# A fused attention and two-layer MoE kernel: the last six w1 tiles decoded two keys later and written into the ring, sums of tokens moved to VectorE, first copies to ScalarE

## The chip, the cores and the metric

The kernel runs on one core of a Trainium2 chip. Its engines work side by side, each through its own list of instructions in order: TensorE (PE, matrix products, with its weight loads shown as PEld), VectorE (DVE), ScalarE (ACT), GpSimd (POOL) and SyncE (SP), which issues the DMAs here. Results of TensorE land in PSUM, in eight banks, and are read from there by VectorE or ScalarE. The metric is the device time of one execution in microseconds (us), as a median over runs.

## The reference

```python
def reference(q, k, v, w1, b1, w2, moe_*, moe2_*):
    # attention: 4 batches, 8 heads, 576 positions, 64 per head
    bias = relu(log-relative position @ w1 + b1) @ w2
    a = softmax(q @ k.T / 8 + bias) @ v          # -> x: 2304 tokens x 512
    # MoE1: 512 -> 768 -> 512
    h = np.maximum(np.maximum(x @ moe_w1, x @ moe_w2), x @ moe_w3)
    x = h @ moe_w_out
    # MoE2: 512 -> 2048 -> 512
    h = x @ moe2_w_in
    g = np.where(h > 0, h, np.exp(np.minimum(h, 0)) - 1)
    return g @ moe2_w_out
```

The weights of both MoE layers are float64 on input. The tokens and weights of the MoE layers are each split into a high and a low half, so that one product of the reference is three matmuls (high by high, high by low, low by high).

## The kernel before, in words

Attention fills roughly the first third of the time, MoE1 comes next, MoE2 after it. The text below is on the stretches that the change touches.

**Decoding weights.** A weight tile (128 x 512 numbers of 64 bits) comes from DRAM as `raw` (`fetch`, L346, two buffers), is put together to float32 by five VectorE instructions (L395, L398, L400, L402, L405) and one of ScalarE (L397) in `decoder`, and is split in `split` into a high half (ScalarE, `hi_of`, L74) and a low half (POOL, `lo_of`, L80). The list `DQ` (L330 to L334) gives the order of the tiles, called keys here: 18 tiles of w1 (the three inputs' matrices of MoE1, six blocks m by three matrices w), six of `wo` (MoE1's output), then those of MoE2 (`wi`, `w3`). Tiles of `wo` stay in SBUF. A tile of w1 normally goes to a buffer `sp`, from there by a store to DRAM (`scw_w_m_w`, L441, issued when another one is queued, in `store`), and, each time it is needed, by a load from there (`load_w`, L468) into a ring `wr` of six buffers `w_t`. There is one exception: where the key is the very next one to be loaded and the ring has room (`direct` in `split`), the halves are written straight into the ring; the key is noted in `HERE`, and its `load_w` issues no DMA. It is stored all the same, for the later passes.

**MoE1** makes three passes over the w1 tiles, one for each 768 tokens, 18 steps each. A step (L600 to L616) calls `load_w` for the tile four steps ahead, `moe1_mm` (24 matmuls, L495) and `moe1_ev`, which evicts the product from PSUM (ScalarE copy L505, VectorE maximum L507) and pumps the decoder, one key a step. There are four pairs of PSUM banks, so the product of step i waits for the eviction of step i-4.

**MoE2** goes through 24 units, eight slices of the hidden layer for three blocks of 768 tokens; the matrix products of the units after the second use sums and differences of token parts (`comb`: `first` computes `e`, L652, and `d`, L653; then d + e, L655; the high half, ScalarE; the low half, VectorE, L80), so that fewer matmuls are needed. In the first two units (n < 2) the sums aren't there yet, and each unit does four plain products, called q here, of 12 matmuls (L666), in turn into the banks Y and X (`bk`). Each q is followed by a copy `c_t` out of PSUM, a `step` for the pieces of ELU that wait (L696 on VectorE; then the high half `gh` on ScalarE and the low half `gl` on POOL, L80), `elu` (Relu, L688, and Exp, L689, on ScalarE), in the second unit by output products of the unit before (three groups of three matmuls, L710), and by two of the sixteen functions of the four sums. From the third unit on, copies and sums `p1`, `c11`, `q1` take products out of the banks; the sums for blocks 1 and 2 are made on the way, in eight more combs.

**The end of a block.** `store_out` copies the six accumulators of output (128 tokens x 512) from PSUM to SBUF, on VectorE and ScalarE in turn, and issues the DMA to `out` (L719); the sixth is copied and stored in two halves.

The order within these stretches is that of the code (`tc.manual_schedule`).

Of the kernel before, what the change touches and what calls it, by code (L numbers as in the profile page):

```python
# [15 lines left out]
ALU = mybir.AluOpType  # L16
# [36 lines left out]
def fused_kernel(ctx, tc, tkq, vv, lt, pk, wm1, wo1, win2, wo2, out):  # L53
    nc = tc.nc
# [15 lines left out]
    def hi_of(eng, dst, src):  # L70
        if eng == "p":
            nc.gpsimd.tensor_scalar(dst, src, 1.0, 1.0, op0=ALU.mult, op1=ALU.mult)
        elif eng == "a":
            nc.scalar.activation(dst, src, AF.Copy)  # L74
        else:
            nc.vector.tensor_copy(dst, src)  # L76

    def lo_of(eng, dst, src, hi):
        e = nc.gpsimd if eng == "p" else nc.vector
        e.tensor_tensor(out=dst, in0=src, in1=hi.bitcast(F32), op=ALU.subtract)  # L80
# [43 lines left out]
    with ExitStack() as pro:  # L124
# [18 lines left out]
        with tc.manual_schedule():  # L143
# [38 lines left out]
            for A in range(36):  # L182
# [9 lines left out]
                o = bt.tile([128, 576], F32, tag="o", name="o_t")  # L192
# [5 lines left out]
                c, r = divmod(A, 8)  # L198
# [130 lines left out]

    DQ = []  # L330
    w1s, wos = [("w1", m, w) for m in range(NM1) for w in range(3)], [("wo", kk, 0) for kk in range(NM1)]
    DQ += w1s[:12] + wos[:3] + w1s[12:] + wos[3:]
    for f in range(NU):
        DQ += [("wi", f, 1), ("wi", f, 0), ("w3", f, 0), ("w3", f, 1)]  # L334
    RAW = {}
# [17 lines left out]
    SCW, WO, HERE, WS, WN = {}, [], set(), [], [0, 0]  # L353
# [75 lines left out]
    todo, late = [], []  # L429

    def splits():

        for fn in late.pop(0) if late else ():
            fn()

    def store():
        if not todo:
            return
        key, sp2, c0 = todo.pop(0)
        d = dram.tile([128, 2, 512], F32, name=f"scw_{key[0]}_{key[1]}_{key[2]}")  # L440
        nc.sync.dma_start(d[:, :, c0:], sp2.bitcast(F32)[:, :, c0:])  # L441
        SCW[key] = d

    dec = decoder()
# [6 lines left out]
    def need(key):  # L451
        while key not in SCW:
            if any(k[0] == key for k in todo):
                store()
            elif late:
                splits()
            else:
                next(dec)

    def load_w(key):  # L460
        need(key)
        if key in HERE:
            HERE.remove(key)
            return
        WN[0] += 1
        t = wr.tile([128, 2, 512], F32R, tag="w", name="w_t")
        c0 = 256 if key[0] == "wi" and key[2] == 3 and key[1] > 1 else 0
        nc.sync.dma_start(t.bitcast(F32)[:, :, c0:], SCW[key][:, :, c0:])  # L468
        WS.append((key, t))

    def take_w(key):
        k, t = WS.pop(0)
        WN[1] += 1
        assert k == key
        return t[:, 0], t[:, 1]
# [44 lines left out]
    for s, (n, c) in enumerate(steps):  # L520
        o = {nm: s + off for nm, off in OFF.items()}
# [48 lines left out]
    for i, (blk, f) in enumerate(units + [(3, 0)]):  # L570
        a = [("wi", f, p) for p in range(4)] if blk < 3 else []
        w = [("w3", units[i - 1][1], p) for p in range(2)] if i else []
# [65 lines left out]
    def x_part(blk, j, t):  # L638
        t0 = blk * TB + t * NB
        return tuple(z[:, 2 * j:2 * j + 2, t0:t0 + NB] for z in (XH, XL))  # L640

    def comb(blk, i):
        a = partial(x_part, blk, *{1: (0, 1), 2: (1, 1), 3: (1, 1), 4: (1, 0)}[i])
        b = {1: partial(x_part, blk, 0, 0), 2: lambda: TT[blk, 1], 3: partial(x_part, blk, 0, 1),
             4: lambda: TT[blk, 2]}[i]
        tt, f = nc.vector.tensor_tensor, F32

        def first():
            t = mp.tile([128, 2, 2, NB], F32R, tag=f"t{i}", name=f"tt{i}", bufs=2 if i < 4 else 1)
            d, e = (mp.tile([128, 2, NB], F32, tag=g, name=f"{g}_t", bufs=1) for g in "de")  # L650
            x, y = a(), b()
            nc.gpsimd.tensor_tensor(out=e, in0=x[1].bitcast(f), in1=y[1].bitcast(f), op=ALU.subtract)  # L652
            tt(out=d, in0=x[0].bitcast(f), in1=y[0].bitcast(f), op=ALU.subtract)  # L653
            TT[blk, i] = (t[:, 0], t[:, 1])
            fns[1:] = [lambda: tt(out=d, in0=d, in1=e, op=ALU.add), lambda: hi_of("a", t[:, 0], d),  # L655
                       lambda: lo_of("v", t[:, 1], d, t[:, 0])]

        fns = [first, None, None, None]
        return [lambda j=j: fns[j]() for j in range(4)]
# [9 lines left out]
    def small(tag, bufs):  # L669
        return mp.tile([128, NB], F32, tag=tag, name=f"{tag}_t", bufs=bufs)  # L670

    def keep(tag, ps, eng):
        t = small(tag, 1)
        hi_of(eng, t, ps)
        return t
# [23 lines left out]
    def step():  # L699
        for p in [p for p in pend]:  # L700
            p.pop(0)()
            if not p:
                pend.remove(p)
# [8 lines left out]
    def store_out(blk, t):  # L712
        o = mp.tile([128, 512], F32, tag="o", name="o_t", bufs=4)
        r0 = blk * TB + 128 * t
        w = 256 if t == 5 else 512
        for c0 in range(0, 512, w):
            cs = slice(c0, c0 + w)
            hi_of("a" if t % 2 else "v", o[:, cs], acc[t][:, cs])
            nc.sync.dma_start(out[r0:r0 + 128, cs], o[:, cs])  # L719

    acc = PAIR[0] + PAIR[1] + PAIR[2]
# [10 lines left out]
    with tc.manual_schedule():  # L732
        for n, u in enumerate(units + [None]):
            pre = units[n - 1] if n else None
            if u:
                blk = u[0]
                GT[u] = [(mp.tile([128, TB], F32R, tag=f"gh{i}", name="gh"), mp.tile([128, TB], F32R, tag=f"gl{i}", name="gl"))
                         for i in range(2)]
                B11, B12, B21, B22 = (x_part(blk, j, t) for j in range(2) for t in range(2))
            if n < 2:  # L740

                for i in range(2):
                    w = take_w(("wi", u[1], 3 * i))
                    v = take_w(("w3", pre[1], i)) if pre else None
                    for q, (b, d) in enumerate(((B11, B21), (B12, B22))):
                        ps = (Y, X)[q]
                        prod(ps, w, 0, b, True, False)
                        prod(ps, w, 1, d, False, True)
                        c = small("c", 4)
                        hi_of("v", c, ps)  # L750
                        step()
                        elu(u, i, q, c)
                        if pre:
                            outs(pre, i, range(3 * q, 3 * q + 3), v)
                        for _ in range(2):
                            sums.pop(0)()
                    loads(2 if pre else 1)
                continue
            if u is None:
                for i in range(2):  # L760
                    step()
                    outs(pre, i, range(6), take_w(("w3", pre[1], i)))
                continue
            w = take_w(("wi", u[1], 0))
            prod(Y, w, 0, B11, True, False)
            p1 = keep("p1", Y, "v")
            step()
            v = take_w(("w3", pre[1], 0))
            outs(pre, 0, (0, 1), v)
            prod(X, w, 1, B21, True, True)  # L770
            loads(1)
            c11 = plus(X, p1)
            step()
            elu(u, 0, 0, c11)
            outs(pre, 0, (2, 3), v)
            w = take_w(("wi", u[1], 1))
            prod(Y, w, 0, TT[blk, 2], False, False)
            q1 = keep("q1", Y, "v")
            step()
            outs(pre, 0, (4, 5), v)  # L780
            loads(1)
            prod(X, w, 1, TT[blk, 1], True, False)
            p5 = keep("p5", X, "a")
            step()
            loads(1)
            v = take_w(("w3", pre[1], 1))
            outs(pre, 1, (0,), v)
            w = take_w(("wi", u[1], 2))
            prod(Y, w, 0, TT[blk, 3], False, False)
            u3 = keep("u3", Y, "v")  # L790
            step()
            outs(pre, 1, (1,), v)
            prod(X, w, 1, B22, False, True)
            c12 = plus(X, q1)
            step()
            elu(u, 0, 1, c12)
            c22 = plus(u3, p5)
            outs(pre, 1, (2, 3), v)
            w = take_w(("wi", u[1], 3))
            prod(Y, w, 1, TT[blk, 4], False, True)  # L800
            c21 = small("c", 4)
            hi_of("v", c21, Y)
            step()
            elu(u, 1, 1, c22)
            elu(u, 1, 0, c21)
            outs(pre, 1, (4, 5), v)
            loads(3)
            if blk < 2:
                if u[1] >= NU - 4:
                    pend.append(comb(blk + 1, u[1] - NU + 5))  # L810
# [65 lines left out]
```

## Time and profile before

| | |
|---|---|
| median of three runs | 1024.46 us (1024.25, 1024.46, 1029.13) |
| profiled execution, device time | 1025.84 us |
| its span, first to last instruction | 1023.9 us |
| mean granted clock of TensorE | 0.994 |
| TensorE busy | 1003.1 us (98%) |
| VectorE, ScalarE, POOL busy | 701.9, 547.5, 353.1 us |
| first pass of MoE1 | its products end near 410.7 us |
| first two units of MoE2 | products and outputs from 635.4 to about 662.5 us |

An engine's busy time says what share of the span it works; where it stands idle, the list of waits names the instruction that waited and what released it. The chain of waits follows the end of the program backwards, at each step to what released the instruction. A granted clock of 1.00 is TensorE's full 2.4 GHz, 0.5 is 1.2 GHz; a value between is a mean of both over the stretch.

### The profile page before, as it was taken

What the parts mean: (1) busy time and instruction counts of PE and PEld (TensorE: products, weight loads), DVE (VectorE), ACT (ScalarE), POOL (GpSimd) and SP (SyncE); (2) the same over time, 40 slices, a digit from 0 to 9 for tenths busy, and PEclk for the clock granted to TensorE, in tenths of its full rate; (3) what the DMA queues carried; (4) which work ended last, traced back from release to release, by engine and by line L of the source; (5) the groups of instructions that cost most, each with busy time, mean ns of one, the idle gap of its engine ahead of it and who ended that gap; (6) DMA issues with size and microseconds to landing.
All of it is one profiled execution on the core that took longest, in us unless ns stands there. A gap on an engine that the chain in (4) does not pass through costs nothing.

```text
span 1023.9 us, 17230 instructions
## 1 busy us (share of the span) xinstructions
PE 1003.1 (98%) x6068; PEld 836.8 (82%) x6068; DVE 701.9 (69%) x1402; ACT 547.5 (53%) x1175; POOL 353.1 (34%) x319
## 2 busy tenths in 40 slices
PE   7999999999999998999999999999999999999998
PEld 3456666666667898999999999889889989989896
DVE  7967877877876698887987962844775356753332
ACT  8978888888886233333333331444445345453443
POOL 0013333333332343534443550522452233522222
PEclk9989999999999999999999999999999999999999
DMA  7741724536332378869977990346567555575562
GB/s 266 267 166 63 248 84 171 160 124 208 124 109 93 124 243 276 303 215 346 319 279 249 324 319 6 113 139 200 178 193 266 182 186 181 193 258 191 171 202 103
DMA packets 68597, 200.80 MB, mean 196 GB/s; under 512 B 9376, under 2 KB 16416, under 8 KB 68512
## 3 DMA queue, kind: packets, MB, share of 16 engines
q1 hardware_dynamic: 68512, 199.70, 57.5%
q8 instruction: 49, 0.80, 0.3%
q14 instruction: 36, 0.29, 0.1%
HBM read 151.31 MB, written 48.37 MB: 195 GB/s over the span
## 4 chain that ended last, share of the span: by engine, by line
PE 92%; DVE 3%; DMA 3%; ACT 1%; issue 0%; SPq 0%; ACTq 0%; DVEq 0%
PE bk L666 16%; PE pb L710 12%; PE pb L495 10%; PE bk L495 9%; PE pb L224 8%; PE bk L299 7%; PE bk L710 6%; PE bk L257 4%; PE bk L590 4%; PE pb L590 4%; PE bk L269 3%; PE pb L186 2%; PE pbb L186 2%; PE pb L226 2%; PE bk L302 2%; DMA scw_w<-sp 2%
## 5 line engine op out<-in xcount | busy, mean ns | idle before, releaser
L80 POOL TENSOR_TENSOR gl<-t_t,gh 128x384 fp32r<-128x384 f32 x96 | 109.0, 1146 | 245.2 <-ACT gh L74 240.0
L250 POOL TENSOR_SCALAR e_t<-e_t,st_t 128x576 f32<-128x576 f32 x64 | 65.8, 1028 | 224.0 <-DVE st_t L244 208.6
L233 DVE CUSTOM_DVE_ANT_0 e_t<-pb,b_t 128x576 f32<-128x576 f32 x144 | 104.0, 756 | 51.3 <-PE pb L224 33.4
L74 ACT ACTIVATE p<-bk 128x512 f32<-128x512 f32 (+2 forms) x224 | 99.0, 473 | 53.0 <-PE bk L257 52.5
L495 PE MATMUL pb<-xh,w_t 128*128 128x384 f32 x448 | 117.2, 337 | 3.8 <-DMA w_t<-scw_w 3.8
L710 PE MATMUL pb<-w_t,gh 128*128 128x512 f32 x384 | 120.1, 394 | 0.0
L238 ACT ACTIVATE e_t<-e_t,st_t 128x576 f32<-128x576 f32 x144 | 111.8, 776 | 1.8 <-DVE st_t L233 1.8
L688 ACT ACTIVATE t_t<-c_t 128x384 f32<-128x384 f32 x96 | 50.0, 521 | 112.6 <-DVE c_t L679 87.2
L495 PE MATMUL bk<-xh,w_t 128*128 128x384 f32 x416 | 108.9, 337 | 0.8 <-ACT xf L320 0.6
L666 PE MATMUL bk<-tt,w_t 128*128 128x384 f32 x528 | 107.4, 338 | 0.0
L666 PEld LDWEIGHTS bk<-tt,w_t 128*128 128x128 f32 x528 | 95.1, 188 | 7.5
L666 PE MATMUL bk<-xh,w_t 128*128 128x384 f32 x328 | 95.7, 338 | 3.6 <-DVE c_t L76 3.6
L495 PEld LDWEIGHTS pb<-xh,w_t 128*128 128x128 f32 x448 | 81.1, 188 | 4.8 <-issue 2.9
L224 PE MATMUL pb<-kq_t 64*128 64x288 f32 x512 | 83.1, 437 | 1.0 <-DVE st_t L233 1.0
L710 PEld LDWEIGHTS pb<-w_t,gh 128*128 128x128 f32 x384 | 71.1, 189 | 6.7
L495 PEld LDWEIGHTS bk<-xh,w_t 128*128 128x128 f32 x416 | 75.4, 188 | 1.2 <-ACT xf L320 0.7
L299 PE MATMUL bk<-p,tv_t 128*64 128x320 f32 (+1 forms) x512 | 76.0, 418 | 0.0
L710 PE MATMUL pb<-w_t,gl 128*128 128x512 f32 x192 | 75.7, 394 | 0.0
L495 PE MATMUL pb<-xl,w_t 128*128 128x384 f32 x224 | 75.2, 336 | 0.0
L74 ACT ACTIVATE gh<-t_t 128x384 fp32r<-128x384 f32 x96 | 48.9, 518 | 46.3 <-DVE t_t L696 46.3
L696 DVE SCALAR_TENSOR_TENSOR t_t<-t_t,c_t 128x384 f32<-128x384 f32 x96 | 71.2, 759 | 0.3 <-issue 0.3
L224 PEld LDWEIGHTS pb<-kq_t 64*128 64x128 f32 x512 | 46.2, 190 | 29.0 <-issue 9.7
(116 smaller groups left out, 2134.7 us busy)
## 6 DMA issues: line engine op xcount, KB each, us to landing
w_t<-scw_w SPq DMA_DIRECT2D x96, 512.0 KB, 4.4
w_t<-scw_wi SPq DMA_DIRECT2D x74, 512.0 KB, 4.2
scw_w<-sp SPq DMA_DIRECT2D x28, 512.0 KB, 5.7
scw_wi<-sp SPq DMA_DIRECT2D x26, 512.0 KB, 4.6
raw<-wo SPq DMA_DIRECT2D x22, 512.0 KB, 4.8
scr<-o_t SPq DMA_DIRECT2D x36, 288.0 KB, 3.8
kq_t<-tkq SPq DMA_DIRECT2D x16, 640.0 KB, 4.4
raw<-wm SPq DMA_DIRECT2D x18, 512.0 KB, 3.9
```

Source lines behind the costliest of these rows:

```text
L74: nc.scalar.activation(dst, src, AF.Copy)
L80: e.tensor_tensor(out=dst, in0=src, in1=hi.bitcast(F32), op=ALU.subtract)
L224: mm(PB[h][:, o], t[r, 640 + 128 * c:768 + 128 * c], t[r, k0:k0 + 288], start=True, stop=True)
L233: nc.vector.tensor_tensor_reduce(out=E[s][:, 576 * h:576 * h + 576], in0=PB[h][:, 224:800], in1=BT[n // 4, c, h], op0=ALU.add, op1=ALU.min ...
L238: nc.scalar.activation(e, e, AF.Exp, bias=st[:, h:h + 1], scale=-1.0, accum_out=st[:, 2 + h:3 + h])
L250: nc.gpsimd.tensor_scalar(e, e, r, 1.0, op0=ALU.mult, op1=ALU.mult)
L299: mm(XO[64 * h:64 * h + 64, 0:w], v[:, 128 * k + 64 * h:128 * k + 64 * h + 64], ps[h][:, k, :], start=(k == 0), stop=False, skip_group_che ...
L495: mm(ps[blk][:, 0:NB], wt[:, ks], xt[:, kk, t0:t0 + NB], start=(j == 0), stop=(j == 11))
L590: mm(ps[blk][:, 0:NB], WO[0][:, kk, wt, ms], xt[:, bs], start=(j == 0), stop=(j == 3 * NM1 - 1))
L666: mm(ps, w[wt][:, ks], b[xt][:, kk], start=(start and j == 0), stop=(stop and j == 5), skip_group_check=True)
L696: pend.append([lambda: nc.vector.scalar_tensor_tensor(out=t, in0=t, scalar=-1.0, in1=c, op0=ALU.add, op1=ALU.max), last])
L710: mm(acc[t], g[:, ts], w[k], start=(f == 0 and i == 0 and j == 0), stop=(f == NU - 1 and i == 1 and j == 2))
```

## The change

1. `DQ`: two `wo` tiles (3 and 4) are decoded ahead of w1's blocks m = 4 and 5, so these six tiles come two keys later. `load_w` no longer decodes on until a tile is stored; a tile in `HERE` is enough.
2. `comb`'s `e` is computed on VectorE, not on POOL (all twelve combs).
3. In the first two units of MoE2 the copies `c_t` go to ScalarE, and the sixteen functions of the sums are called one after each q in the first unit and three in the second, not two and two.
4. `store_out`: the fifth output tile is copied and stored in halves too; the first halves of the fifth and sixth go to VectorE, the second ones to ScalarE.

```diff
--- before.py
+++ after.py
@@ -329,7 +329,7 @@
 
     DQ = []
     w1s, wos = [("w1", m, w) for m in range(NM1) for w in range(3)], [("wo", kk, 0) for kk in range(NM1)]
-    DQ += w1s[:12] + wos[:3] + w1s[12:] + wos[3:]
+    DQ += w1s[:12] + wos[:5] + w1s[12:] + wos[5:]
     for f in range(NU):
         DQ += [("wi", f, 1), ("wi", f, 0), ("w3", f, 0), ("w3", f, 1)]
     RAW = {}
@@ -458,7 +458,13 @@
                 next(dec)
 
     def load_w(key):
-        need(key)
+        while key not in HERE and key not in SCW:
+            if any(k[0] == key for k in todo):
+                store()
+            elif late:
+                splits()
+            else:
+                next(dec)
         if key in HERE:
             HERE.remove(key)
             return
@@ -649,7 +655,7 @@
             t = mp.tile([128, 2, 2, NB], F32R, tag=f"t{i}", name=f"tt{i}", bufs=2 if i < 4 else 1)
             d, e = (mp.tile([128, 2, NB], F32, tag=g, name=f"{g}_t", bufs=1) for g in "de")
             x, y = a(), b()
-            nc.gpsimd.tensor_tensor(out=e, in0=x[1].bitcast(f), in1=y[1].bitcast(f), op=ALU.subtract)
+            tt(out=e, in0=x[1].bitcast(f), in1=y[1].bitcast(f), op=ALU.subtract)
             tt(out=d, in0=x[0].bitcast(f), in1=y[0].bitcast(f), op=ALU.subtract)
             TT[blk, i] = (t[:, 0], t[:, 1])
             fns[1:] = [lambda: tt(out=d, in0=d, in1=e, op=ALU.add), lambda: hi_of("a", t[:, 0], d),
@@ -712,10 +718,10 @@
     def store_out(blk, t):
         o = mp.tile([128, 512], F32, tag="o", name="o_t", bufs=4)
         r0 = blk * TB + 128 * t
-        w = 256 if t == 5 else 512
+        w = 256 if t > 3 else 512
         for c0 in range(0, 512, w):
             cs = slice(c0, c0 + w)
-            hi_of("a" if t % 2 else "v", o[:, cs], acc[t][:, cs])
+            hi_of("a" if t % 2 and t < 5 or c0 else "v", o[:, cs], acc[t][:, cs])
             nc.sync.dma_start(out[r0:r0 + 128, cs], o[:, cs])
 
     acc = PAIR[0] + PAIR[1] + PAIR[2]
@@ -747,12 +753,12 @@
                         prod(ps, w, 0, b, True, False)
                         prod(ps, w, 1, d, False, True)
                         c = small("c", 4)
-                        hi_of("v", c, ps)
+                        hi_of("a", c, ps)
                         step()
                         elu(u, i, q, c)
                         if pre:
                             outs(pre, i, range(3 * q, 3 * q + 3), v)
-                        for _ in range(2):
+                        for _ in range(3 if pre else 1):
                             sums.pop(0)()
                     loads(2 if pre else 1)
                 continue
```

The order of the instructions moves in three places. The first is SP's queue in the first pass of MoE1; `scw_w_4_0` is tile m = 4, w = 0 in DRAM, `sp` the decoded tile, `w_t` a ring buffer. Before:

```order
L468 DMA w_t<-scw_w_3_2_3693 128x1024
L441 DMA scw_w_4_0_3997<-sp_3920 128x1024
L346 DMA raw<-wm 128x1024
L468 DMA w_t<-scw_w_4_0_3997 128x1024
L441 DMA scw_w_4_1_4040<-sp_3966 128x1024
L346 DMA raw<-wm 128x1024
L468 DMA w_t<-scw_w_4_1_4040 128x1024
L441 DMA scw_w_4_2_4089<-sp_4010 128x1024
```

After:

```order
L474 DMA w_t<-scw_w_3_2_3693 128x1024
L346 DMA raw<-wm 128x1024 x2
L441 DMA scw_w_4_0_4079<-w_t 128x1024
L346 DMA raw<-wm 128x1024
L441 DMA scw_w_4_1_4122<-w_t 128x1024
L346 DMA raw<-wm 128x1024
L441 DMA scw_w_4_2_4163<-w_t 128x1024
L346 DMA raw<-wo 128x1024
L441 DMA scw_w_5_0_4210<-w_t 128x1024
```

The loads of the six tiles (L468) are gone, and the stores read the ring buffer.

The second is ScalarE at the start of MoE2; `xh` is the last work of MoE1, `tt` the high half of a sum, `bk` a PSUM bank. Before:

```order
L596 ACTIVATE xh<-pb_99 128x384 x2
L688 ACTIVATE t_t<-c_t 128x384
L689 ACTIVATE t_t<-t_t 128x384
L688 ACTIVATE t_t<-c_t 128x384
L689 ACTIVATE t_t<-t_t 128x384
L74 ACTIVATE tt_6602<-d_t 128x768
L74 ACTIVATE gh<-t_t 128x384
```

After:

```order
L602 ACTIVATE xh<-pb_99 128x384 x2
L74 ACTIVATE c_t<-bk_865 128x384
L694 ACTIVATE t_t<-c_t 128x384
L695 ACTIVATE t_t<-t_t 128x384
L74 ACTIVATE c_t<-bk_866 128x384
L694 ACTIVATE t_t<-c_t 128x384
L695 ACTIVATE t_t<-t_t 128x384
L74 ACTIVATE c_t<-bk_865 128x384
L74 ACTIVATE gh<-t_t 128x384
L694 ACTIVATE t_t<-c_t 128x384
L695 ACTIVATE t_t<-t_t 128x384
L74 ACTIVATE tt_6590<-d_t 128x768
```

The copies `c_t` stand on ScalarE now, and the first sum's high half comes after three of them.

The third is VectorE at the same place; `xl` is the last work of MoE1 there. Before:

```order
L597 TENSOR_TENSOR xl<-pb_99,xh 128x384 x2
L76 COPY c_t<-bk_865 128x384
L653 TENSOR_TENSOR d_t<-xh 128x768
L655 TENSOR_TENSOR d_t<-d_t,e_t 128x768
L76 COPY c_t<-bk_866 128x384
L696 SCALAR_TENSOR_TENSOR t_t<-t_t,c_t 128x384
L80 TENSOR_TENSOR tt_6602<-d_t,tt_6602 128x768
L76 COPY c_t<-bk_865 128x384
L696 SCALAR_TENSOR_TENSOR t_t<-t_t,c_t 128x384
L653 TENSOR_TENSOR d_t<-xh,tt_6602 128x768
```

After:

```order
L658 TENSOR_TENSOR e_t<-xl 128x768
L603 TENSOR_TENSOR xl<-pb_99,xh 128x384
L659 TENSOR_TENSOR d_t<-xh 128x768
L603 TENSOR_TENSOR xl<-pb_99,xh 128x384
L702 SCALAR_TENSOR_TENSOR t_t<-t_t,c_t 128x384
L661 TENSOR_TENSOR d_t<-d_t,e_t 128x768
L702 SCALAR_TENSOR_TENSOR t_t<-t_t,c_t 128x384 x2
L80 TENSOR_TENSOR tt_6590<-d_t,tt_6590 128x768
L702 SCALAR_TENSOR_TENSOR t_t<-t_t,c_t 128x384
L658 TENSOR_TENSOR e_t<-xl,tt_6590 128x768
```

The copies are gone from VectorE, `e_t` is new there, and the sums stand behind one another with an ELU piece between.

## Rows read from the trace of the kernel before

**Rows 1.** The page's first part: busy us (share of the span), instructions.

```profile
PE 1003.1 (98%) x6068; PEld 836.8 (82%) x6068; DVE 701.9 (69%) x1402; ACT 547.5 (53%) x1175; POOL 353.1 (34%) x319
```

**Rows 2.** TensorE's waits, whole span: total us, times, longest us.

```profile
PE pb L495 <- DMA w_t<-scw_w: 3.8, 2, 2.2
PE bk L666 <- DVE c_t L76: 3.6, 4, 2.0
```

**Rows 3.** Stretches: length; busy PE, PEld, DVE, ACT, POOL (instructions); clock, DMA, GB/s.

```profile
380.00:390.00 10.00, 10.00 (x60) 10.00 (x59) 8.84 (x13) 2.68 (x5) 3.63 (x3) 1.00 0.87 304
390.00:410.00 20.00, 16.07 (x90) 15.20 (x89) 17.63 (x25) 7.77 (x14) 7.52 (x6) 1.00 0.83 279
665.00:670.00 5.00, 2.98 (x10) 2.67 (x10) 3.47 (x5) 2.19 (x4) 1.32 (x2) 0.75 0.05 17
670.00:1016.00 346.00, 346.00 (x1719) 311.27 (x1719) 178.00 (x273) 150.93 (x303) 115.98 (x98) 1.00 0.58 191
```

**Rows 4.** The chain of waits, 366 to 411 us: start us, us, what.

```profile
365.85 6.94 PE pb L495 x40
...
372.89 5.26 DMA scw_w<-sp
...
378.59 5.28 DMA scw_w<-sp
...
402.61 3.59 DMA w_t<-scw_w
```

**Rows 5.** TensorE in order of time: start, us, instruction [idle before <-releaser].

```profile
399.69 0.42 PE L495 MATMUL pb<-xh,w_t 128*128 128x384 f32 x1 [1.53 <-DMA w_t<-scw_w]
```

**Rows 6.** POOL in order of time, first pass of MoE1.

```profile
396.50 1.29 POOL L80 TENSOR_TENSOR wo_t<-t_w,wo_t 128x512 fp32r<-128x512 f32 x1 [3.28 <-ACT wo_t L74]
```

**Rows 7.** VectorE in order of time, first pass of MoE1.

```profile
396.77 1.31 DVE L395 TENSOR_SCALAR x_t<-raw 128x512 int32<-128x512 int32 x1 [1.01 <-DMA raw<-wo]
...
406.40 0.54 DVE L507 TENSOR_TENSOR a_t<-bk,a_t 128x384 f32<-128x384 f32 x1
```

**Rows 8.** VectorE in order of time, start of MoE2.

```profile
638.08 0.95 DVE L653 TENSOR_TENSOR d_t<-xh 128x768 f32<-128x768 f32 x1
...
644.61 2.62 DVE L653 TENSOR_TENSOR d_t<-xh,tt 128x768 f32<-128x768 f32 x1
...
666.54 0.55 DVE L76 COPY c_t<-bk 128x384 f32<-128x384 f32 x1
```

**Rows 9.** POOL in order of time, start of MoE2.

```profile
644.23 2.18 POOL L652 TENSOR_TENSOR e_t<-xl,tt 128x768 f32<-128x768 f32 x1
...
671.90 1.02 POOL L80 TENSOR_TENSOR gl<-t_t,gh 128x384 fp32r<-128x384 f32 x1 [1.05 <-ACT gh L74]
```

**Rows 10.** The chain of waits, 634 to 674 us.

```profile
635.43 2.09 PE bk L666 x12
...
667.14 1.99 PE bk L666 x6
669.13 2.27 PE pb L710 x6
671.39 1.06 PE bk L666 x6
672.46 1.39 PE bk L710 x6
```

**Rows 11.** Groups of instructions, 635 to 671 us: busy us, mean ns, idle before.

```profile
L688 ACT ACTIVATE t_t<-c_t 128x384 f32<-128x384 f32 x8 | 4.2, 525 | 17.8 <-DVE c_t L76 17.8
...
L74 ACT ACTIVATE tt<-d_t 128x768 fp32r<-128x768 f32 x4 | 3.3, 828 | 0.0
```

**Rows 12.** ScalarE in order of time, third unit of MoE2.

```profile
674.93 0.49 ACT L74 ACTIVATE p_t<-bk 128x384 f32<-128x384 f32 x1 [2.02 <-PE bk L666]
```

**Rows 13.** VectorE in order of time, a late sum.

```profile
750.89 0.54 DVE L679 TENSOR_TENSOR c_t<-bk,p_t 128x384 f32<-128x384 f32 x1
```

**Rows 14.** ScalarE in order of time, the end.

```profile
1019.96 0.66 ACT L74 ACTIVATE o_t<-bk 128x256 f32<-128x256 f32 x2 [0.85 <-DMA out<-o_t]
```

## The prediction

> **What bounds the kernel now.** I began with the busy times: TensorE (PE) works 1003.1 of 1023.9 us, VectorE (DVE) 69%, ScalarE (ACT) 53% [rows 1]. So an edit pays only where it shortens a stretch in which PE stands still. The list of stalls names two such places that the diff touches: L495, in the first pass of MoE1, waits 3.8 us in two stalls for a w1 tile that comes from DRAM, and L666, at the start of MoE2, waits 3.6 us in four stalls for `c_t`, the copy that VectorE makes out of PSUM [rows 2]. The busy times by stretch give both places their size: PE lacks 20.00 - 16.07 = 3.93 us in 390-410; in 665-670 it is busy 2.98 of 5 us at a granted clock of 0.75; and from 670 to 1016 us it never pauses, 346.00 of 346.00 [rows 3]. Nothing done there can win time; it can only lose some.
>
> The first place. The chain of waits runs through SyncE's queue: the store of a decoded tile takes 5.26 and 5.28 us to land, and only then may that tile's load (3.59) be issued [rows 4]. What is written behind the waiting load on SP, the next store among it, waits with it: stores issue at 372.89 and 378.59, one tile in 5.7 us, while PE uses one tile (24 of the 40 matmuls that took 6.94 us) in 4.16 us [rows 4]. With four tiles of lead it runs dry for tiles 16 and 17.
>
> The second place. In the first two MoE2 units a "q" is 12 matmuls into one of two banks, 2.09 us [rows 10], and the bank is free again when `c_t` is copied. The copy stands in VectorE's queue behind the sums: the one at 666.54, for a product that had ended near 660.5, came behind a `d_t` and an add. A `d_t` took 0.95 us where POOL was idle; 2.62 belongs to one that began 0.4 us after POOL's `e_t` of 2.18 us [rows 8, 9]. VectorE is not slow there by itself: it stands still until POOL's instruction ends.
>
> **The change, part by part.** The sum is made against the profiled execution, 1025.84 us (span 1023.9). The median of the runs, 1024.46, is 1.4 below it, and I subtract the same gains from that.
>
> *w1's last six tiles.* Two keys later, each is decoded when the next load in line is its own, so ACT and POOL write it into the ring, and six loads leave SP's queue. The stores stay, but nothing on SP now waits for their landing. Tile 17 takes the place that `wo` tile 4 had in the decoding, whose low half POOL finished at 396.50 + 1.29 = 397.8 [rows 6]. PE was ready for tile 16 at 399.69 - 1.53 = 398.2 [rows 5], so without stalls it wants tile 17 at about 402: 4 us of margin, and more for tiles 12 to 16. What is late next? VectorE evicts every product and decodes one key a step. Its eviction of step 14 ended at 406.40 + 0.54 = 406.9, after five waits for raw tiles of up to 1.01 us (3.05 together) [rows 7], which the blocked SP queue had delayed; without those I put it at 403.8, and the product that reuses the bank (step 18) is wanted at 406.1. The other candidate is the second pass's first tile: its load stands on SP behind a raw tile that waits for the decoder (about 397.5); with 3.59 us for such a load and some queueing it is there at 402.5 to 404, against the same 406.1. Both margins are 2 us or more. Gain: 3.93 us of PE's busy time, 4.1 with the restarts. I take **4.0**; bounds 0 (a new limit at the old pace) and 4.1.
>
> *First copies on ScalarE, sums on VectorE.* ACT's work for a q is a copy of 0.49 [rows 12], and Relu, Exp and `gh` at 0.53 each, 2.08 us, with 0.83 more for one of the four high halves [rows 11]; PE takes 2.09 us for a q in unit 0 and 4.16 in unit 1, where three output tiles are added. What a copy can wait for is a high half ahead of it in ACT's queue, which waits for VectorE's add; a bank is wanted again only after one whole other q, so up to 4.16 us of that is hidden in unit 1. How much there is to win: without stalls the stretch would be 8 x 2.09 + 4 x 2.07 (outputs) + 4.86 (the first half of unit 2, two products of 1.05 and two groups of outputs of 1.38) = 29.9 us from 635.43, so the first product from the sums would start at 665.3; it starts at 671.39 [rows 10]. Those 6.1 us are the 3.6 of the stalls, 1.8 of granted clock (after the 2.0 us stall six matmuls took 1.99 instead of 1.06 and the next six 2.27 instead of 1.39 [rows 10]) and 0.7 of restarts. What is late next: VectorE's chain. In unit 1 it does three sums (0.95 for each of their four operations on 768 floats, so 3.8 when not held up), four ELU steps of 0.54, and stands still for some five `gl` of POOL at 1.02 [rows 7 to 9]: 11.4 + 2.2 + 5.1 = 18.7, with 2.8 for three waits on high halves 21.5 us. It has 4 x 4.16 + 4.86 = 21.5. That is a stall between 0 and 1.5 us; I take 0.4: gain **5.7**, bounds 2 (two copies as late as the one before 667.14) and 6.1.
>
> A two-input sum of VectorE ran 2.62 us beside POOL's `e_t`, and 0.95 alone [rows 8, 9]. The Trainium skill, "SBUF — State Buffer", section "SBUF: two separate sides", calls the port pair of VectorE and GpSimd an exclusive lock: one of the two stands still for the whole of the other's instruction. This trace agrees: the excess of 1.67 us is what was left of `e_t`. By that rule the five `gl` still hold the chain up and the gain is 5.7; if the port were merely shared, they would cost nothing and it would be 6.1.
>
> *Sums on VectorE later on.* Eight more sums (blocks 1 and 2) put 0.95 us each on VectorE's queue and take 2.18 from POOL's. VectorE works 178 of 346 us in that time [rows 3]. Its nearest deadline is `c11`, finished at 751.43 [rows 13], some 0.6 us before its bank is used again, and in a place where the sum before it was held up by POOL. Taking `e_t` from POOL removes more from that chain than it adds: 0 (bounds +0.3, and -8 x 0.6 = -4.8 if `c11` came later by twice its margin each time).
>
> *The end.* Output tile 4 is cut into halves as tile 5 was, and the halves go to VectorE and ACT in turn. ACT's two copies ended at 1020.6 [rows 14]; VectorE's now run beside them, but an eighth DMA has to be issued, and SP's issues come last. I take **0.1** (bounds -0.3 and +0.4).
>
> Sum: 4.0 + 5.7 + 0.1 = 9.8. The profiled execution would be 1016.0, the median 1024.46 - 9.8 = **1014.7**.
>
> **Rivals.** (1) *MoE1 stays at the old pace*, because VectorE, or the raw tiles with their two buffers, decide it and not SP's loads. For it speaks that VectorE is busy 8.84 of 10 us in 380-390, before any stall; against it that PE is at 10.00 there [rows 3]. 4.0 are not won: 1018.7. (2) *ACT's queue in VectorE's place*: three copies stand behind high halves that wait for adds, and each is 1.4 us later than the bank is wanted (a `gl` and some waiting for it): 4.2 lost of 6.1, 1018.5. For it speaks that ACT now carries both; against it the 4.16 us of cover. (3) Both: 1022.5. (4) *The other side: the same queue with dearer waits.* If the adds come so late that each of unit 1's four copies leaves PE idle for some 2.2 us, the granted clock falls behind each as at 667.14 (1.8 us): 4 x (2.2 + 1.8) = 16.0 lost against 4.0 + 6.1 + 0.1 won, 1030.3. It decides from the point where VectorE's chain takes 21.5 + 4 x 2 = 29.5 us; I find 21.5. That the change does nothing is excluded for MoE1: six loads are missing from SP's rows.
>
> **How the numbers follow.** Forecast 0.73, (1) 0.10, (2) 0.08, (3) 0.05, (4) 0.04. The range reaches up to cases (1) and (2), 1018.8, and down to the full gains, 4.1 + 6.1 + 0.4, with 0.5 for scatter, 1013.4; (3), (4) and part of the forecast's own spread are left out. 0.5% is 5.1 us, about what a measurement of this kernel can tell from no change, so faster means below 1019.3: the forecast, (1) and half of (2), 0.87; the same 0.09; slower 0.04.
>
> **What would show it.** Right: no stall of L495 for `w_t` near 400; stalls of L666 in 635-670 below 1 us together, a granted clock of 1.00 there and `d_t` near 0.95; the first product from the sums some 9.7 us earlier; PE still without a pause after it. Wrong: L495 waiting for `a_t` of VectorE or for `w_t` of POOL (rival 1); `c_t` on ACT beginning long after its product, with a `tt` ahead of it (rivals 2 to 4); new gaps near the eight later sums. The weakest term is the 0.4 for VectorE's chain.

## The result and the profile after

| | before | after |
|---|---|---|
| median | 1025.3 us of 6 runs (1024.2 to 1029.13) | 1014.77 us of 6 runs (1012.82 to 1016.41) |
| ratio | | 0.9883, 95% interval 0.9859 to 0.9908 |
| profiled execution | 1025.84 us, span 1023.9 | 1015.60 us, span 1013.8 |

The change is faster. The median after is the forecast to 0.1 us, but that is luck, and it comes from the base: the three runs of before that I subtracted from had a median of 1024.46, six have 1025.3. By the ratio, the gain is 1.17% or 12.0 us (9.4 to 14.4), and 1024.46 x 0.9883 = 1012.5 lies 0.9 us below the low end of my range; the interval goes from 1010.0 to 1015.0. The pair of profiled executions differs by 10.2 us. So the mechanisms stood, and the gain was more than the 9.8 that I had summed up. What was too small, and why, is the question of the experiments.

The page's first part after, against [rows 1]:

```profile
PE 999.9 (99%) x6068; PEld 835.1 (82%) x6068; DVE 688.8 (68%) x1409; ACT 551.1 (54%) x1183; POOL 330.1 (33%) x307
```

TensorE's list of waits after, against [rows 2] (total us, times, longest):

```profile
PE pb L186 <- ACT f_t L165: 6.5, 1, 6.5
PE pb L224 <- DVE st_t L233: 1.3, 2, 0.9
PE bk L257 <- DVE e_t L252: 0.9, 2, 0.5
PE bk L501 <- ACT xf L320: 0.6, 1, 0.6
```

Neither place is left: no wait for `w_t`, none for `c_t`. What remains lies in the attention part and, for the 0.6 us of `xf`, early in MoE1; the same waits were there before. The busy times of stretches after, against [rows 3] (length; busy PE, PEld, DVE, ACT, POOL with instructions; granted clock, DMA share, GB/s):

```profile
390.00:410.00 20.00, 20.00 (x118) 20.00 (x116) 19.34 (x28) 7.92 (x15) 9.71 (x7) 1.00 0.69 223
632.00:662.00 30.00, 30.00 (x160) 28.05 (x159) 23.90 (x28) 18.98 (x39) 8.73 (x8) 1.00 0.33 104
662.00:1006.00 344.00, 344.00 (x1713) 309.56 (x1712) 170.06 (x280) 150.69 (x302) 100.11 (x89) 1.00 0.59 192
```

TensorE is busy all of the time in all three, at a granted clock of 1.00.

For a size that doesn't depend on how idle time is counted, I take three marks in TensorE's timeline, the first matmul of MoE1, the first of MoE2 and the first on a sum (`tt`). They stand in rows of their own; before:

```profile
322.45 0.44 PE L495 MATMUL pb<-xh,w_t 128*128 128x384 f32 x1
...
635.27 0.33 PE L666 MATMUL bk<-xh,w_t 128*128 128x384 f32 x1
...
671.23 0.70 PE L666 MATMUL bk<-tt,w_t 128*128 128x384 f32 x3
```

and after:

```profile
323.08 0.44 PE L501 MATMUL pb<-xh,w_t 128*128 128x384 f32 x1
...
631.55 0.33 PE L672 MATMUL bk<-xh,w_t 128*128 128x384 f32 x1
...
661.24 1.05 PE L672 MATMUL bk<-tt,w_t 128*128 128x384 f32 x5
```

The stretch of MoE1 went from 312.82 to 308.47 us (4.35 less), the first two units of MoE2 from 35.96 to 29.69 (6.27 less). From there to the last matmul it is 347.88 and 347.85, and from that to the end of the span 4.79 and 4.71. The start was 0.6 us later after (323.08 against 322.45), hence 10.1 in the span. These two stretches, called M and S below, are what I compare in all profiles.

### The profile page after: what moved, and what is told of

It reads as the page before. It is cut to its first block, busy times and chain, and to the rows that moved or that the text cites. A ratio compares the mean times of both kernels' runs of the same rounds, so it can differ in the third digit from the quotient of the medians.

```text
span 1013.8 us, 17221 instructions
## 1 busy us (share of the span) xinstructions
PE 999.9 (99%) x6068; PEld 835.1 (82%) x6068; DVE 688.8 (68%) x1409; ACT 551.1 (54%) x1183; POOL 330.1 (33%) x307
## 4 chain that ended last, share of the span: by engine, by line
PE 98%; DVE 1%; DMA 1%; issue 0%; ACT 0%; SPq 0%; DVEq 0%; ACTq 0%
PE bk L672 18%; PE pb L716 13%; PE pb L501 12%; PE bk L501 11%; PE pb L224 8%; PE bk L299 7%; PE bk L716 6%; PE bk L257 4%; PE bk L596 4%; PE pb L596 4%; PE bk L269 3%; PE pb L186 3%; PE pbb L186 2%; PE pb L226 2%; PE bk L302 2%; PE bk L273 1%
## 5 line engine op out<-in xcount | busy, mean ns | idle before, releaser
L224 PEld LDWEIGHTS pb<-kq_t 64*128 64x128 f32 x512 | 45.8, 189 | 29.5 <-issue 9.2
L501 PE MATMUL bk<-xl,w_t 128*128 128x384 f32 x208 | 69.9, 336 | 0.0
```

Source lines behind the costliest of these rows:

```text
L224: mm(PB[h][:, o], t[r, 640 + 128 * c:768 + 128 * c], t[r, k0:k0 + 288], start=True, stop=True)
L501: mm(ps[blk][:, 0:NB], wt[:, ks], xt[:, kk, t0:t0 + NB], start=(j == 0), stop=(j == 11))
```

## The experiments

Theory: the two stalls are separate and are worth what their stretch loses; the parts add up. Rival: the gain beyond my sum comes from elsewhere, from a part that does more than end its stall. The first four kernels ran on one chip with 20 runs of before (median 1025.36).

**The first pass alone.**

```diff
-    DQ += w1s[:12] + wos[:3] + w1s[12:] + wos[3:]
+    DQ += w1s[:12] + wos[:5] + w1s[12:] + wos[5:]
...
     def load_w(key):
-        need(key)
+        while key not in HERE and key not in SCW:
...
```

> Only the order of the decoded tiles and the shorter load are changed (the first part of the change). Theory A (the parts add, each by its stall): the two L495 waits for a tile from DRAM go, 4.1 us, ratio 0.9960, and the start of MoE2 stays as before with its four waits for c_t and a granted clock under 1. Theory B (the parts are worth more than their stalls, since the measured gain of the whole, 12 us by the ratio, is above the sum of 9.8): over 5 us here. If VectorE's decoding set the pace, 0 to 1 us.

Measured: 1020.71 us, ratio 0.9947 (0.9927 to 0.9967), a gain of 5.4 us (3.4 to 7.5). TensorE is busy 40.00 of 40 us between 380 and 420, and MoE2 starts as before. Its waits:

```profile
PE bk L672 <- DVE c_t L76: 3.7, 4, 2.1
PE pb L224 <- DVE st_t L233: 1.2, 2, 0.8
PE pb L501 <- DMA w_t<-scw_w: 0.8, 1, 0.8
PE bk L672 <- DVE p_t L76: 0.7, 1, 0.7
```

Two things differ from what I expected. In this execution two tiles came late in the second and third pass, by 0.79 and 0.55 us, and M was 310.85, not 308.3; in the whole change, whose MoE1 is the same, no such wait was seen. Four of the nine executions of this kernel took 1018.03 to 1018.42 us at the same mean clock as the profiled one (0.999), so the late tiles of its profile are not the rule. And at the start of MoE2 the same four waits, 3.7 us, were there without a fall of the granted clock; in its place `p_t`, the copy behind the fourth sum, came 0.7 us late.

**The start of MoE2 alone.**

```diff
-            nc.gpsimd.tensor_tensor(out=e, in0=x[1]...
+            tt(out=e, in0=x[1]...
...
-                        hi_of("v", c, ps)
+                        hi_of("a", c, ps)
...
-                        for _ in range(2):
+                        for _ in range(3 if pre else 1):
```

> Only the start of MoE2 and the sums are changed (e on VectorE, copies on ScalarE, one and three functions of the sums after a product). Theory A: 6.1 us, ratio 0.9940, no stall of TensorE between the start of MoE2 and the end of its work, the two L495 waits as before. Theory B: over 7 us, with time won outside these stretches. My own forecast had 5.7 here, with 0.4 us of stall left.

Measured: 1017.56 us, ratio 0.9922 (0.9903 to 0.9941), a gain of 8.0 us (6.0 to 9.9). S is 29.68 us, and no wait is left in it: 6.3 us less than before. My 0.4 us of rest did not come. By its time this kernel meets theory B (over 7 us), but the interval does not exclude 6.1, and the spans of the two profiles (1016.6 and 1023.9 us) differ by 6.3 from S and 2.3 from an earlier start of MoE1 (320.17 against 322.45 us), less 1.3 in MoE1. The earlier start is the granted clock in attention, which between 60 and 70 us was 0.66 in the profile of before and 1.00 in this one; more on that with the whole. MoE1 has no edit here, yet its stretch was M = 314.08, 1.3 longer than in the profile of before, with three waits for a tile instead of two worth naming:

```profile
PE pb L495 <- DMA w_t<-scw_w: 3.8, 2, 2.7
PE bk L495 <- DMA w_t<-scw_w: 1.4, 1, 1.4
```

**The halves of the output alone.**

```diff
-        w = 256 if t == 5 else 512
+        w = 256 if t > 3 else 512
...
-            hi_of("a" if t % 2 else "v", ...
+            hi_of("a" if t % 2 and t < 5 or c0 else "v", ...
```

> Only the copies and stores of the fifth output tile are changed. Theory A: 0.1 us within 0.4 either way, ratio 0.9996 to 1.0004, and the span after the last matmul 7.4 to 7.5 us as before. Theory B: 1 us or more.

Measured: 1025.39 us, ratio 0.9997 (0.9980 to 1.0013): nothing that can be measured. The end of its span after the last matmul is 4.89 us (before 4.79; the whole change 4.71 in both of its profiles; the other kernels 4.75 to 4.85), so even the 0.1 us is within the scatter. As this kernel is before in everything that comes earlier, its profile is a second sample of before, and it shows what the first had not. Stretches of it:

```profile
390.00:400.00 10.00, 7.97 (x46) 7.48 (x44) 7.50 (x12) 3.88 (x7) 3.75 (x3) 1.00 0.74 219
400.00:410.00 10.00, 6.70 (x33) 6.31 (x33) 7.60 (x12) 2.51 (x5) 3.29 (x3) 0.91 0.79 284
410.00:420.00 10.00, 10.00 (x55) 10.00 (x54) 9.72 (x16) 4.10 (x8) 6.41 (x5) 0.92 0.94 342
```

The stalls take 2.03 + 3.30 = 5.3 us of TensorE's time, not 3.9, and after the last one the granted clock falls (0.91 and 0.92), which it did not in the profile of before. M is 315.79 us, 3.0 more. The first of the three waits is for tile 15:

```profile
395.72 0.41 PE L495 MATMUL bk<-xh,w_t 128*128 128x384 f32 x1 [2.03 <-DMA w_t<-scw_w]
```

Its load was issued at 389.93; before, at 389.61, and there the tile was in the ring 4.1 us later, here 5.8. What made the load slower is not settled.

**The whole again.** No edit beside the change.

> The whole change again, beside the other three on one chip. Theory A: the sum of the three within 0.5 us, 10.2 to 10.4 us, ratio 0.9900, with what the earlier comparison had above it (12 us, interval 9.4 to 14.4) due to executions in which TensorE's granted clock does not fall in attention near 60 to 70 us; those are 2 to 3 us shorter, of the kernel before as of this one. Theory B: 12 us in executions of equal granted clock.

Measured: 1014.88 us, ratio 0.9886 (0.9865 to 0.9906): 11.7 us (9.6 to 13.8), the first comparison again. M is 308.18 and S 29.68. Its span is 1010.7 us, 3.1 less than that of the profile after: the granted clock between 60 and 70 us, in attention, was 1.00 here and 0.66 there, which the rows say (after first, then this one):

```profile
60.00:70.00 10.00, 9.45 (x39) 6.13 (x38) 6.24 (x22) 6.11 (x16) 2.32 (x3) 0.66 0.37 135
...
60.00:70.00 10.00, 9.35 (x60) 6.41 (x60) 8.06 (x27) 8.75 (x23) 3.97 (x4) 1.00 0.57 201
```

In both, TensorE had stood idle 0.9 us before 58.1 and 0.4 us before 60.4. That fall came in 5 of the 14 profiles, with the change and without it, and costs about 2.4 us where it comes: MoE1's first matmul stands at 322.45 to 323.08 us in those five and at 319.98 to 320.71 in the other nine. It isn't part of the gain, but how often it falls in a handful of executions moves a median.

The mean clock of a profile tells it (0.993 to 0.996 in the five, 0.997 to 1.000 in the nine), so I can compare executions without it: 16 of before with a mean clock of 0.998, median 1024.0 us, and five of the change with 0.999 or 1.000, median 1012.8. That is 11.2 us, an estimate over several chips and few executions: between theory A's 10.2 to 10.4 and theory B's 12. So my theory that such executions hold all of the excess fell: they hold at most a part of it, and the rest is in M. By the rows the parts add up: S is 29.68 us with the second part alone and in the whole, and M of the order alone, which comes below, is 308.16, that of the whole. The times are too coarse to show it, 5.4 + 8.0 + 0.3 = 13.7 us against 11.7, with intervals of some 2 us to each side.

**The three edits of MoE2's start, one by one and two by two.** These ran together, with 19 runs of before (median 1025.33). The edits are those of the second experiment's diff, each alone, and then the copies and the spread without the move of `e`.

> Of the change only e on VectorE instead of POOL. Theory A (the queue decides: the copies stay behind the sums on VectorE, and a sum with its two copies and two ELU steps takes 8.3 to 8.8 us there, not 8.8 to 9.1): TensorE still waits for c_t, 2.5 to 3.5 us of its idle time at the start of MoE2 are left of 3.6, gain 0.5 to 2 us. Theory B (POOL's e decides, because VectorE stands still beside it): the waits go but for 1 us, gain 4 to 6 us.

> Of the change only the first copies on ScalarE; e stays on POOL, two functions of the sums after each product. Theory A (the copy's queue decides): the four waits for c_t are gone, at most 1.5 us of idle time is left where the first product from the sums waits for p_t, the copy behind the fourth sum; gain 4.5 to 6 us. Theory B (POOL's e decides): VectorE's adds come as late as before, ScalarE's high halves wait for them, and the copies behind them leave TensorE 2 to 4 us idle; gain 0 to 2 us.

> Of the change only the spread of the sums, one function after each product of the first unit and three in the second. Theory A: VectorE has the same work before the same product, and the copies in the second unit stand behind three functions; 3 to 6 us of idle time, no gain within 1.5 us either way. Theory B (the first unit's rate was the fault): idle time below 1.5 us, gain 3 us or more.

> The start of MoE2 as in the change, but with e left on POOL. Theory A: no waits for c_t; VectorE's chain in the second unit is longer by three times 1.7 us (d beside e) and POOL's gl stand behind e, so the first product from the sums waits 2 to 5 us for p_t; gain 1 to 4 us, less than with the copies alone. Theory B (e's place matters nothing once copies are on ScalarE): 6.1 us.

TensorE's waits in these stretches, in that order:

```profile
PE bk L666 <- DVE c_t L76: 2.3, 3, 1.0
...
PE bk L666 <- DVE p_t L76: 0.7, 1, 0.7
```

```profile
PE bk L666 <- DVE p_t L76: 0.7, 1, 0.7
```

```profile
PE bk L666 <- DVE c_t L76: 1.4, 1, 1.4
...
PE bk L666 <- DVE p_t L76: 1.0, 1, 1.0
```

```profile
PE bk L666 <- DVE p_t L76: 1.7, 1, 1.7
```

| edit | ratio | S, us |
|---|---|---|
| before (profiles with this start) | 1 | 35.24 to 35.96 |
| `e` on VectorE | 0.9971 (0.9951 to 0.9990) | 33.65 |
| spread one and three | 0.9967 (0.9950 to 0.9984) | 32.46 |
| copies on ScalarE | 0.9935 (0.9911 to 0.9959) | 30.49 |
| copies and spread | 0.9965 (0.9949 to 0.9981) | 31.51 |
| `e` and copies | 0.9955 (0.9935 to 0.9975) | 29.68 |
| all three | 0.9922 (0.9903 to 0.9941) | 29.68 |

S is the sharper measure here; the ratios hold MoE1's scatter too. The queue decides: the copies on ScalarE bring 5 of the 6 us alone, and ScalarE's high halves, waiting for adds that POOL's `e` delays, hold no copy up so long that TensorE would notice. Moving `e` alone helps little, because the copies still stand behind the sums. The third kernel contradicts what I expected: the spread alone wins 3 us, with 2.4 us of idle time left, so neither of its theories holds whole. That it wins since the first unit, with 2.09 us of TensorE for a q, has to carry less is argued from the order of the work; no run shows it by itself. But beside the copies it does harm (31.51 against 30.49) as long as `e` is on POOL: what is late is then only the fourth sum, and the spread puts more of the sums late (argued too; the wait for `p_t`, behind the fourth sum, is 1.7 us instead of 0.7).

**`e` and the copies, without the spread.** This one and the next three ran with 12 runs of before (median 1024.38).

> The start of MoE2 with e on VectorE and the copies on ScalarE, but two functions of the sums after each product as before. The copies alone left 0.65 us of idle time, before the first product from the sums. Theory A (that rest is the chain of sums on VectorE, and POOL's e prolongs it): no idle time, gain 6 to 7.5 us, and the spread of one and three adds nothing. Theory B (the spread is needed to have the fourth sum in time): 0.5 to 1.5 us of idle time left at p_t.

Measured: ratio 0.9955 (0.9935 to 0.9975), S 29.68 with no idle time. So the spread adds nothing to the change. The gain of 6 to 7.5 us did not show in the time, 4.6 us (2.6 to 6.7): M was 314.05 in its profile, with a fall of the granted clock in MoE1, and the interval does not exclude 6.3.

**w1 first.** The other way to be in time: all w1 tiles earlier, still through DRAM.

```diff
-    DQ += w1s[:12] + wos[:3] + w1s[12:] + wos[3:]
+    DQ += w1s + wos
```

> Only the decoding order, and the other way round: all 18 w1 tiles first, then wo, so the last six are decoded three keys earlier than before and still stored, and loaded back from DRAM. Theory A (the load on SP waits for the landing of a store issued just ahead of it, and everything behind it on the queue waits too): the store has landed long before the load is due, the L495 waits shrink from 3.8 us and more to under 1.5 us though all six loads remain; gain 3 to 5.5 us. Theory B (the traffic of the six stores and loads, 0.5 MB each, is the cost): the waits stay at 3.5 us or more, no gain within 1.5 us.

Measured: ratio 0.9965 (0.9950 to 0.9979), a gain of 3.6 us (2.2 to 5.1), M 308.63: the stalls are gone but for one of 0.2 us, though all six loads are still there. The waits of SP's queue (SPq) for the landing of a store, in total, times and longest, here:

```profile
SPq L468 <- DMA scw_w<-sp: 4.8, 1, 4.8
```

and before:

```profile
SPq L468 <- DMA scw_w<-sp: 26.4, 6, 5.8
```

Five of six are gone. So it is the waiting on SP's queue for a store issued too late, and neither the six loads nor their traffic, that made MoE1 stall. How much of the stall is the late tile itself and how much what stood behind the waiting load, this kernel doesn't separate, as it ends both. Going straight into the ring is one way to end it, not the only one.

**The order without the edit of the load**, and **the order one key later** (with that edit):

```diff
-    DQ += w1s[:12] + wos[:3] + w1s[12:] + wos[3:]
+    DQ += w1s[:12] + wos + w1s[12:]
```

> Only the order of the change (two wo tiles ahead of w1's last six), with the load as before, which decodes on until the tile is stored. Theory A (the order makes the tile the next one to be loaded, so it goes into the ring; the edit of the load only spares decoding ahead): no load of the six on SP, no L495 wait for a tile, gain 4 to 5.5 us as in the first experiment. Theory B (the edit of the load is needed): decoding one key ahead in one go delays VectorE's evictions, L495 waits for a_t, 2 to 4 us of idle time near 385 to 425.

> The order moved one key further than in the change: all six wo tiles ahead of w1's last six, with the load of the change. In the change tile 17's low half is done at 396.8 us, wanted at about 402.5, and a key takes VectorE 4.2 to 4.8 us. Theory A (margin about 5 us): one key later leaves 0 to 1.5 us, no stall or one of under 1 us, gain 4 to 5.5 us. Theory B (the margin is smaller, since the last tile's halves and the eviction share VectorE): stalls of 1 to 4 us at tile 16 and 17.

Measured: 0.9952 (0.9935 to 0.9968), 4.9 us, with M 308.16, and 0.9958 (0.9942 to 0.9973), 4.3 us, with M 308.74. The order alone does it; the edit of the load is not needed for the gain. One key later, the last tile's low half is done 3.4 us later (counted from the first matmul of MoE1), no tile is waited for, and the one stall of the stretch names the eviction, not the tile:

```profile
PE pb L501 <- ACT a_t L511: 0.3, 1, 0.3
```

So the margin of 4 us in the prediction was not too large: even with those 3.4 us used up, tile 17 is done at 397.8 us and wanted only at about 400.5, one tile after the matmul that stalled (396.31). No version beats the whole change: in it neither stretch has idle time left.

## Why the prediction was right or wrong

**What bounds the kernel**: right. The two stalls that the list of waits named were all that the change could reach; ending both took each stretch to the length without stalls, and the 348 us after it stayed 348.

**MoE1, the step that failed: the size, 4.0 with a bound of 4.1.** The mechanism is shown (the six loads, SP's wait, w1 first). But I read the price of the stall off one execution, and set its upper bound by that execution's own idle time. In the eight profiles whose MoE1 is that of before, M is 312.64 to 315.79, mean 313.9; the profile I had (312.82) is the second shortest. With the change it is 308.47 and 308.18, and 310.85 in the first experiment. That makes 4.7 us as the mean of those three, 5.6 as that of the whole's two, and single executions up to 7.6. In the pair of profiles alone it is 4.35, over my bound already. Above 308.3, the mean of the whole's two, the rows hold three parts:

- the stalls for tiles 15, 16 and 17 together, 3.6 to 5.5 us in the eight, where I had 3.9 from one: tile 15 comes late too (0.2 us before; 0.3 to 2.0 in six of the other seven);
- 0.5 to 0.6 us that are not in the stalls, in the five profiles whose clock stays up there, where I had 0.2 for restarts;
- some 1.5 us more in the three profiles in which the granted clock falls after a stall there (2.0 to 2.2 us with the part before), where I had nothing.

One of the eight lists its longest stall, 3.64 us in the kernel with `e` alone, under VectorE's eviction `a_t`:

```profile
405.77 0.41 PE L495 MATMUL pb<-xh,w_t 128*128 128x384 f32 x1 [3.64 <-DVE a_t L507]
```

That isn't rival (1): the stall began at 402.1, the eviction had ended at 399.7, and tile 17's load was issued only at 402.09:

```profile
399.11 0.55 DVE L507 TENSOR_TENSOR a_t<-pb,a_t 128x384 f32<-128x384 f32 x1
```

```profile
402.09 0.32 SPq L468 DMA_DIRECT2D w_t<-scw_w  x1
```

The stall is what is left between a load's landing and the moment when TensorE wants the tile, so it takes up the whole scatter of the landings: tile 15's load took 4.1 us in one profile and 5.8 in another. Why it does, no run shows. A bound from one execution should have been open above.

**The margins of MoE1**: right, in part by luck. After, POOL ends tile 17's low half at 396.8, where I had 397.8, and VectorE the eviction of step 14 at 404.1, where I had 403.8:

```profile
394.94 1.82 POOL L80 TENSOR_TENSOR w_t<-t_w,w_t 128x512 fp32r<-128x512 f32 x1 [2.09 <-ACT w_t L74]
```

```profile
403.54 0.55 DVE L513 TENSOR_TENSOR a_t<-bk,a_t 128x384 f32<-128x384 f32 x1
```

Counted from the first matmul of MoE1, which came 0.6 us later after, tile 17 was 1.7 us earlier than I had it, and wanted at about 402.5: a margin of 5.7 us, not 4. My 403.8 took off five waits for raw tiles, 3.05 us; the last of them, 0.56 us before 407.50, comes after the eviction that it was to delay, so four with 2.5 us were there to be won, and the closeness is luck:

```profile
407.50 0.43 DVE L395 TENSOR_SCALAR x_t<-raw 128x512 int32<-128x512 int32 x1 [0.56 <-DMA raw<-win]
```

After, VectorE is busy 19.34 of 20 us there, without the waits for raw tiles, and TensorE doesn't see it.

**MoE2, 5.7 forecast, 6.27 in the pair of profiles.** The upper bound of 6.1 was nearly the truth for that pair; the 0.4 of rest was wrong. VectorE's chain was shorter than 21.5 us: from the second unit's first matmul (631.6 + 8.4 = 640.0) to the end of `p_t` (660.3) it took 20.3. VectorE, POOL and ScalarE there, after:

```profile
643.74 1.77 DVE L659 TENSOR_TENSOR d_t<-xh,tt 128x768 f32<-128x768 f32 x1
...
648.29 1.79 DVE L658 TENSOR_TENSOR e_t<-xl 128x768 f32<-128x768 f32 x1
...
651.87 1.37 DVE L702 SCALAR_TENSOR_TENSOR t_t<-t_t,c_t 128x384 f32<-128x384 f32 x1
...
655.77 1.37 DVE L702 SCALAR_TENSOR_TENSOR t_t<-t_t,c_t 128x384 f32<-128x384 f32 x1
...
659.79 0.55 DVE L76 COPY p_t<-bk 128x384 f32<-128x384 f32 x1
```

```profile
643.23 1.47 POOL L80 TENSOR_TENSOR gl<-t_t,gh 128x384 fp32r<-128x384 f32 x1 [0.74 <-ACT gh L74]
```

```profile
646.53 0.85 ACT L74 ACTIVATE tt<-d_t 128x768 fp32r<-128x768 f32 x1 [2.41 <-DVE d_t L661]
647.29 0.48 ACT L74 ACTIVATE c_t<-bk 128x384 f32<-128x384 f32 x1
```

I had five `gl` each holding VectorE up for its whole 1.02 us, and 2.8 us of waits for high halves. It was held up four times by some 0.83 us, 3.3, as each `gl` had begun somewhat earlier; and the waits for high halves were 1.4, as the work between fills them. That is 3.2 us less than I had summed, and the chain is only 1.2 us shorter, because my sum also left something out: until 642.9, when the second sum begins, VectorE finishes the first one (0.96) and waits 0.8 for ScalarE. The `d_t` at 643.74 stood until the `gl` that began at 643.23 and took 1.47 had ended, at 644.70, and then took its 0.8. It cost TensorE nothing here. The Trainium skill calls the port pair that VectorE and GpSimd share an exclusive lock, held for a whole instruction ("SBUF — State Buffer", section "SBUF: two separate sides"). These rows agree with it. ScalarE's queue behaved as forecast: the copy at 647.29 stood behind a high half that had waited 2.41 us, its product had ended near 646.2, so it came 1 us late, and its bank was wanted at 652.3 only.

The split of the 6.1 was wrong, too. I had put 1.8 us of it on the granted clock. In the kernels with the old start whose clock did not fall (four of six), S is 35.24 to 35.27, against 35.96 and 35.85 where it fell. So the fall costs 0.6 to 0.7 us, not 1.8: without it TensorE reaches the first product from the sums earlier and waits there 0.7 us for `p_t`. VectorE's chain sets how early the stretch can end; in the profile of before its `p_t` was there at 670.45, only 0.8 us ahead of TensorE, so most of the clock's loss was hidden under it:

```profile
669.90 0.55 DVE L76 COPY p_t<-bk 128x384 f32<-128x384 f32 x1
```

Where the clock did not fall, the change wins 5.6 us of S. That 5.7 lies so near is luck: the 6.1 held a fall of the clock that comes in two of six profiles, and the 0.4 taken off it never came.

**Later sums and the end**: right, 0 (347.88 and 347.85) and 0.1 (4.79 and 4.71, within scatter).

**The rivals.** (1), (2) and (3) did not come. (4) is not only far off (the chain took 20.3 us of the 29.5 that it needed); its price was wrong as well, since the granted clock does not fall after every wait of 2 us: it fell in two of the six profiles with the 2.0 to 2.1 us wait in MoE2.

**The sum.** My range ended at 1013.4 because it took 4.1 and 6.1 as the most that the two stretches can give; the first of them was too small. With the means of the profiles it would have been 4.7 to 5.6 for MoE1, 5.8 for MoE2 (35.47, the mean of six, less 29.68) and 0 to 0.1: 10.5 to 11.5 us, where the two timed comparisons have 12.0 and 11.7, with intervals of over 4 us, and the executions without the clock's fall in attention 11.2. Whether the last half to one microsecond is scatter, by how often that fall comes, stays open; no stretch of the profiles shows it.

## What to carry to other kernels

The size of a stall that ends a chain of DMA landings was not a constant here (3.6 to 5.5 us in eight profiles): one profile gives a sample of it, and a forecast that removes the stall should leave its upper bound open by what the same landings vary elsewhere in the trace. When a copy out of PSUM waits behind other work, look at the queue in which it stands before making that work faster: the other queue gave 5 of 6 us, the faster work 2. And before charging a stall with the clock that falls after it, ask which chain would end the stretch without the fall.

## What I had not expected of the hardware

The granted clock does not follow from the length of the stall that precedes it. The same kernel had 1.00 between 60 and 70 us in one execution and 0.66 in another after nearly the same waits; after MoE1's longest stall it fell with waits of 2.4 and 2.5 us in two profiles and stayed at 1.00 with waits of 2.2, 2.6, 2.7 and 3.6 us in others, and in a third it fell after tile 15's 2.0 us already, a stall that left it at 1.00 in another. What decides it, no run here shows.
